# A new plan of order for a fused recurrence and expert kernel, with more buffers and one factor kept in PSUM

## The chip, the cores and the metric

The kernel runs on one core of a Trainium2 chip. The metric is the device time of one execution in microseconds, taken as the median of several runs.

## The reference

Two stages are fused. The first is a gated linear recurrence over 768 steps, for 4 batches and 8 heads with head size 48. The second is an expert layer on the 3072 resulting tokens, with 384 model columns and 2048 hidden columns. All inputs and the output are float32.

```python
f = 1.0 / (1.0 + np.exp(-f_logit))
for t in range(S):
    state = f[:, :, t, :, None] * state + np.einsum('bhd,bhe->bhde', k[:, :, t], v[:, :, t])
    y[:, :, t] = np.einsum('bhd,bhde->bhe', q[:, :, t], state)
x = y.transpose(0, 2, 1, 3).reshape(B * S, H * D)
h = x @ w_in
out = (h * (1.0 / (1.0 + np.exp(-h)))) @ w_out
```

## The kernel before

The sequence is cut into 6 chunks of 128 steps. With 4 batches this makes 24 units, numbered 4 x chunk + batch, each with 128 tokens and all 8 heads. A unit passes through these tasks; the short names are those of the plan and of the function `emit`.

- Inputs: `f`, `k`, `q`, `v` load 128 x 384 float32 each, all issued by SyncE's queue (L156) in 1024 pieces of 192 bytes. `wi` and `wo` (four pieces each, L158 and L160) load and convert the weights from GpSimd's queue.
- Gate: `E` and `L` (ScalarE, L162 and L164) make the logarithm of the gate, with opposite sign; `cs` (TensorE, L167, L171) sums it along the chunk into a PSUM bank; `ia`, `a` and `al` (ScalarE, L174, L176, L178) take exponentials of these sums: the factor for k, the factor for q, and the chunk's decay.
- Scaling: `ki` (GpSimd, L183) multiplies k, `qg` (VectorE, L190) multiplies q, `vb` (GpSimd, L185) converts v.
- Attention inside the chunk: the scaled q and k are transposed, either by TensorE and a copy (`tq`, `qkc`, L195 and L197, 13 units) or by one DMA transpose (`qkD`, L200, 11 units); `sc` (L208) forms scores, `at` (VectorE, L214, two halves) masks them, `y` (L220 with the state, L224 with the scores) gives the output.
- State: `d` (L242), `sd` (VectorE, L247 or L249) and `su` (GpSimd, L254) carry the state to the batch's next chunk. The last chunk skips them.
- Hand-over: `yc` (L228) converts the output, and it is transposed by TensorE (`yT`, `xc`, L232 and L234, 13 units) or by DMA (`yD`, L237, 11 units).
- Expert layer: for each of four parts `mi` (12 matmuls, L260) and `si` (ScalarE, Silu, L266), then `mo` (4 matmuls for each part, L271), `oc` (VectorE eviction, L274) and `so` (store by SyncE's queue, L277).

`T.s` and `T.e` load ScalarE's table for Silu and for the exponentials (L306). `Z.n` runs n matmuls on zeros (L309).

The order of all tasks is written out in the string `PLAN`, made by an offline search. A word is task, unit, part and, behind the colon, the buffer slots that it takes: `mi.3.2:4` is part 2 of unit 3's first expert product into PSUM bank 4. Each engine and each queue runs its own tasks strictly in the plan's order; semaphores for data and for the reuse of buffers are added automatically. `SLOTS` says how many buffers there are of each kind; `ps` are the eight PSUM banks. SyncE's queue holds loads, stores and DMA transposes in one order, so that a store waiting for its `oc` also holds the loads that follow it. A bank taken by `cs` is free for the next taker once its last reader is done.

Of the kernel before, what the change touches and what calls it, by code (L numbers as in the profile page):

```python
# [34 lines left out]
si.0.3:0 T.e yT.4:5 mo.1.0:4 xc.4:1 mo.3.0:6 E.7:1 mi.4.3:0 L.7:0 mi.4.2:1 E.5:0 cs.7:2 mi.4.1:7 L.5:1 f.6:7 al.7:5
ia.7:0 mi.4.0:5 a.7:1 mo.2.1:3 mo.1.1:4 mo.3.1:6 k.6:7 mo.1.2:4 ki.7:0 cs.5:2 v.7:5 mo.2.2:3 al.5:0 ia.5:1 q.6:7
mo.3.2:6 a.5:0 T.s qg.5:3 mo.2.3:3 q.10:0 ki.5:3 mo.3.3:6 oc.2:0 q.8:1 si.4.2:2 mo.1.3:4 qg.7:0 si.4.3:2 oc.3:1 so.2
tq.5:2 si.4.1:2 oc.1:2 v.5:6 tq.7:3 si.4.0:2 T.e qkc.5:1 mo.0.0:1 so.1 qkc.7:2 mo.4.0:0 so.3 vb.7:5 q.9:2 sc.5:6,7
E.6:1 sc.7:4,5 at.5.1:2 d.7:2 L.6:2 mo.0.1:1 f.8:0 at.7.0:0 cs.6:3 at.7.1:0 mo.0.2:1 f.10:1 al.6:3 ia.6:2 at.5.0:2
mo.4.1:0 a.6:2 ki.6:1 v.6:7 sd.7:1 y.7:7 qg.6:1 mo.0.3:1 v.10:0 vb.5:0 yc.7:2 mo.4.2:0 su.7:0 oc.0:3 q.11:3 yT.7:4  # L40
y.5:5 xc.7:2 tq.6:3 so.0 yc.5:0 mi.7.0:6 f.9:2 qkc.6:3 yT.5:2 E.8:0 T.s mi.7.1:7 xc.5:3 v.8:1 mi.7.3:1 k.8:0 mi.5.1:4
si.7.0:1 vb.6:3 mi.5.0:5 v.11:3 si.7.3:1 vb.10:2 si.7.1:1 mi.5.3:3 v.9:2 si.5.1:3 mi.5.2:2 si.5.3:3 f.11:3 mi.7.2:6
si.5.0:3 si.5.2:3 k.9:2 sc.6:1,7 si.7.2:1 T.e mo.4.3:0 at.6.0:1 k.10:1 d.5:4 vb.8:1 at.6.1:1 mo.7.0:3 sd.5:0 k.11:3
d.6:5 y.6:2 E.9:1 oc.4:4 mo.7.1:3 su.5:0 L.8:3 yc.6:1 f.12:4 L.9:4 mo.5.0:6 sd.6:1 vb.11:4 E.10:0 so.4 yT.6:1 cs.8:7
su.6:0 L.10:0 xc.6:0 f.16:5 cs.9:4 mo.5.1:6 al.8:2 ia.8:0 al.9:1 vb.9:5 ia.9:1 f.13:6 mi.6.2:0 ki.8:2 a.9:0 mi.6.3:2
a.8:1 T.s k.13:4 qg.9:4 ki.9:4 mi.6.1:5 qg.8:2 f.14:7 mi.6.0:1 si.6.2:0 v.16:4 tq.8:4 si.6.3:0 tq.9:7 qkc.8:0 si.6.0:0
v.13:5 cs.10:0 si.6.1:0 T.e d.8:2 qkc.9:2 mo.7.2:3 f.15:0 sd.8:0 mo.6.0:1 q.12:4 sc.9:4,5 sc.8:7,2 al.10:4 ia.10:2
at.9.0:0 mo.7.3:3 a.10:2 q.16:5 ki.10:0 at.9.1:0 E.11:1 mo.6.1:1 E.13:0 at.8.0:2 k.12:5 mo.5.2:6 L.11:1 at.8.1:2
L.13:2 y.9:4 v.14:6 vb.16:0 oc.7:5 E.14:1 mo.6.2:1 E.12:0 yc.9:2 so.7 y.8:0 vb.13:3 L.14:3 qg.10:0 cs.13:5 k.16:6
L.12:4 yT.9:7 su.8:0 yc.8:0 cs.11:2 al.13:5 tq.10:3 ia.13:0 xc.9:1 q.15:6 al.11:0 yT.8:4 a.11:0 cs.14:0 ki.13:3  # L50
qkc.10:1 mi.9.2:7 a.13:1 f.17:2 xc.8:3 al.14:3 a.14:2 T.s qg.11:1 mi.9.0:3 k.18:7 mi.8.0:5 mi.8.2:4 q.14:7 si.9.2:2
vb.14:1 si.9.0:2 mo.6.3:1 v.19:7 si.8.2:1 mi.8.1:7 oc.6:6 si.8.0:1 q.13:2 cs.12:3 si.8.1:1 mi.9.1:4 so.6 mi.8.3:1
si.9.1:2 q.17:1 sc.10:5,7 si.8.3:1 mi.9.3:4 v.15:0 at.10.1:1 mo.8.0:1 at.10.0:1 si.9.3:2 T.e k.17:0 mo.5.3:6 qg.14:2
k.14:2 y.10:7 oc.5:7 d.13:5 d.9:4 yc.10:1 mo.8.1:1 al.12:2 so.5 ia.11:1 vb.19:5 sd.9:1 ia.12:2 k.15:1 mo.9.0:6 ki.11:1
E.17:1 qg.13:3 yT.10:7 a.12:0 mo.8.2:1 qkD.13:3 su.9:0 xc.10:2 L.17:0 qg.12:4 tq.11:2 ia.14:0 E.16:0 mi.10.2:4 ki.12:4
qkc.11:2 E.15:1 mi.10.1:3 sd.13:0 L.16:2 T.s q.19:0 tq.12:7 mi.10.0:0 v.21:1 qkc.12:0 ki.14:2 mi.10.3:2 si.10.2:0
f.20:1 si.10.0:0 sc.11:5,7 qkD.14:1 si.10.3:0 d.11:4 at.11.1:0 cs.16:0 mo.8.3:1 si.10.1:0 T.e sd.11:1 sc.13:2,7
at.11.0:0 sc.12:3,4 mo.9.1:6 at.13.0:2 q.20:3 al.16:1 a.16:2 at.13.1:2 y.11:5 L.15:1 mo.10.0:2 v.12:3 yc.11:2 su.11:0
ia.16:1 y.13:7 at.12.1:1 E.20:0 f.18:3 yT.11:5 cs.15:0 vb.21:4 yc.13:0 L.20:3 d.10:4 mo.9.2:6 q.18:7 su.13:0 xc.11:0
al.15:0 a.15:1 sd.10:1 ia.15:2 cs.20:7 yD.13:3 mi.11.2:5 at.12.0:1 a.20:0 su.10:0 ia.20:0 T.s oc.8:0 mi.11.0:4 f.22:6  # L60
qg.16:1 mi.11.3:0 vb.12:3 qg.15:3 so.8 ki.16:1 mi.11.1:3 q.21:2 qg.20:0 si.11.0:3 d.12:7 ki.15:3 si.11.2:3 v.22:2
y.12:1 sd.12:0 mi.13.1:4 si.11.3:3 yc.12:1 qkD.16:2 vb.15:2 si.11.1:3 mi.13.3:5 su.12:0 si.13.1:1 yT.12:7 mi.13.0:0
si.13.3:1 xc.12:1 mi.13.2:1 si.13.0:1 qkD.15:3 vb.22:3 mi.12.1:3 si.13.2:1 T.e mi.12.2:4 mi.12.0:7 mi.12.3:5 E.18:1
v.23:4 E.22:0 mo.11.0:0 v.17:5 L.18:4 mo.9.3:6 L.22:2 T.s k.19:4 mo.11.1:0 oc.9:2 f.21:7 cs.18:1 mo.11.2:0 so.9
si.12.3:2 v.18:6 si.12.1:2 d.15:6 mo.11.3:0 sd.15:1 si.12.0:2 k.22:3 sc.16:5,3 si.12.2:2 T.e oc.11:1 sc.14:6,7 k.21:5
mo.10.1:2 at.16.0:0 at.14.0:2 so.11 sc.15:4,0 f.19:4 mo.10.2:2 at.14.1:2 E.21:1 q.23:4 mo.12.0:5 al.18:5 at.15.0:1
a.18:2 L.21:1 y.14:6 at.15.1:1 q.22:5 ia.18:1 mo.10.3:2 yc.14:2 v.20:7 ki.18:4 y.15:7 at.16.1:0 d.16:4 cs.22:0 yD.14:2
yc.15:0 d.14:1 su.15:0 cs.21:6 a.22:1 y.16:3 sd.16:0 ia.21:2 mo.12.1:5 yD.15:0 yc.16:1 a.21:0 vb.18:2 mo.13.0:7
ia.22:1 sd.14:1 su.16:0 yD.16:3 E.19:0 oc.10:3 cs.17:4 mo.13.1:7 L.19:3 qg.21:3 su.14:0 so.10 al.17:4 qg.22:1
mo.12.2:5 a.17:0 k.20:2 qg.18:4 cs.19:6 vb.17:1 qg.17:2 k.23:6 mo.13.2:7 vb.20:0 al.19:2 a.19:1 T.s ki.22:1 mi.14.1:3  # L70
qkD.18:0 mi.16.2:0 ki.21:3 si.14.1:3 mi.16.0:1 si.16.2:0 ki.20:0 mi.16.3:2 si.16.0:0 qkD.21:1 mi.16.1:3 si.16.3:0
mi.14.0:0 si.16.1:0 mi.14.2:1 si.14.0:3 qkD.20:3 mi.14.3:2 si.14.2:3 qg.19:3 mi.15.3:3 si.14.3:3 T.e mi.15.2:0
mi.15.0:1 qkD.22:2 mo.16.0:2 ia.17:1 ia.19:2 T.s ki.17:2 mi.15.1:4 mo.12.3:5 ki.19:3 f.23:2 mo.13.3:7 oc.12:4
si.15.3:2 mo.16.1:2 si.15.1:2 so.12 oc.13:5 si.15.0:2 sc.20:6,5 so.13 sc.18:3,4 si.15.2:2 T.e at.20.1:2 sc.21:7,1
mo.16.2:2 at.18.0:1 mo.15.0:0 at.18.1:1 mo.16.3:2 at.20.0:2 E.23:1 y.18:5 at.21.1:0 y.20:3 L.23:4 qkD.17:0 yc.18:2
d.18:4 d.17:6 vb.23:0 d.19:1 sd.18:0 mo.15.1:0 sd.17:1 su.18:0 cs.23:5 mo.14.0:4 yc.20:0 ia.23:0 at.21.0:0 a.23:2 T.s
mo.15.2:0 ki.23:0 yD.18:1 sd.19:0 mo.14.1:4 oc.16:6 yD.20:3 qg.23:0 sc.17:6,3 sc.22:5,7 at.17.1:1 mo.15.3:0 so.16
at.17.0:1 qkD.19:3 mi.18.1:1 at.22.0:2 mi.18.3:2 at.22.1:2 mi.18.0:3 si.18.1:1 oc.15:7 si.18.3:1 mi.18.2:6 so.15
si.18.0:1 mi.20.1:5 si.18.2:1 y.17:7 si.20.1:0 mi.20.0:1 yc.17:1 su.17:0 qkD.23:0 mi.20.3:0 si.20.0:0 y.22:2 si.20.3:0
# [263 lines left out]
```

## Time and profile before

| | |
|---|---|
| median of 3 runs | 195.94 us (195.77 to 196.79) |
| the profiled execution: its time / its span | 194.64 us / 192.9 us |
| PE / ACT / DVE / POOL busy | 174.1 / 125.4 / 95.7 / 65.6 us |
| weight loads on PE (PEld) busy | 138.2 us |
| input packets under 512 B | 116544 of 123225 |
| read from HBM / written | 25.17 MB / 4.72 MB |
| granted TensorE clock | 0.997 |

The profile shows one execution. A busy time is the time in which an engine worked on something; PE's includes the overlap of its pipeline. An idle stretch is put down to what ended it. The chain that ended last is followed back from the last instruction, step by step, to what released it; its share of the span was 56% for PE, 17% for DMA, 9% for ACT and 7% for the issue of transfers by SyncE's queue.

### The profile page before, as it was taken

The page shows a single profiled execution, that of the slowest core. Times are in us where ns is not written, and L with a number is a line of the kernel's source. Part 1 is how long each engine was busy: PE and PEld are TensorE (multiplying, and loading weights), DVE is VectorE, ACT ScalarE, POOL GpSimd, SP SyncE. Part 2 cuts the span into 40 slices and gives each one's busy share as a digit, 9 for nine tenths or more (in the row PEclk, how much of TensorE's full clock was granted, in tenths as well). Part 3 has the DMA queues.
Part 4 walks back from the last instruction along what each step waited for, and adds up shares of the span by engine and source line. Part 5 has one row for each costly group of instructions (what it writes and reads, how often), then busy time and mean ns, then how long its engine had stood idle before and what let it go on. Part 6 is the DMA issues. An engine that isn't in the chain of part 4 may idle for free.

```text
span 192.9 us, 5771 instructions
## 1 busy us (share of the span) xinstructions
PE 174.1 (90%) x2397; PEld 138.2 (72%) x2397; DVE 95.7 (50%) x182; ACT 125.4 (65%) x234; POOL 65.6 (34%) x104
## 2 busy tenths in 40 slices
...
GB/s 126 209 196 181 159 202 187 185 185 189 233 224 220 184 222 174 213 200 212 218 209 164 204 177 230 215 133 170 181 114 146 131 76 44 27 57 85 0 82 82
DMA packets 123225, 31.07 MB, mean 161 GB/s; under 512 B 116544, under 2 KB 123200, under 8 KB 123200
## 3 DMA queue, kind: packets, MB, share of 16 engines
...
q0 software_dynamic: 3712, 3.15, 10.3%
...
q14 instruction: 7, 0.06, 0.1%
HBM read 25.17 MB, written 4.72 MB: 155 GB/s over the span
## 4 chain that ended last, share of the span: by engine, by line
PE 56%; DMA 17%; ACT 9%; SPq 7%; issue 4%; POOL 2%; DVE 2%; ACTq 0%; DVEq 0%; POOLq 0%
PE ps L260 25%; PE ps L271 23%; SPq L156 7%; DMA v<-in_v_dram 5%; DMA w_in<-in_moe_w_in_dram 4%; ACT hT L266 4%; DMA xT<-yb 3%; DMA f<-in_f_logit_dram 3%; ACT L306 2%; DMA q<-in_q_dram 2%; PE ps L195 2%; PE ps L208 2%; ACT e L162 2%; PE ps L224 1%; DVE qk L190 1%
## 5 line engine op out<-in xcount | busy, mean ns | idle before, releaser
L266 ACT ACTIVATE hT<-ps 128x512 bf16<-128x512 f32 x96 | 54.1, 599 | 38.1 <-PE ps L260 29.4
L260 PE MATMUL ps<-xT,w_in 128*128 128x128 bf16 x1152 | 70.2, 219 | 4.5 <-DMA xT<-yb 2.1
L260 PEld LDWEIGHTS <-w_in 128*128 128x128 bf16 x1152 | 66.0, 98 | 8.9 <-issue 3.1
L271 PE MATMUL ps<-w_out,hT 128*128 128x384 bf16 x384 | 70.3, 326 | 1.8 <-DVE o L274 1.8
L271 PEld LDWEIGHTS <-hT 128*128 128x128 bf16 x384 | 34.7, 97 | 21.7 <-issue 2.0
L183 POOL TENSOR_TENSOR qk<-k,ia 128x384 bf16<-128x384 f32 x24 | 24.5, 1028 | 36.8 <-ACT ia L174 33.4
L214 DVE TENSOR_TENSOR atm<-ps,triu 128x512 bf16<-128x512 f32 x48 | 30.4, 682 | 12.5 <-PE ps L208 12.5
L190 DVE TENSOR_TENSOR qk<-q,a 128x384 bf16<-128x384 f32 x24 | 18.4, 778 | 26.4 <-ACT a L176 14.7
L254 POOL TENSOR_TENSOR st<-sd,al 48x192 bf16<-48x192 f32 x40 | 21.5, 538 | 24.2 <-PE ps L220 20.9
L274 DVE COPY o<-ps 128x384 f32<-128x384 f32 x24 | 13.2, 554 | 32.4 <-PE ps L271 28.5
L306 ACT ACT_TABLE_LOAD x21 | 26.9, 1283 | 0.4
L185 POOL CAST vb<-v 128x384 bf16<-128x384 f32 x24 | 13.0, 549 | 32.2 <-DMA v<-in_v_dram 25.9
L162 ACT ACTIVATE e<-f 128x384 f32<-128x384 f32 x24 | 12.1, 523 | 9.9 <-DMA f<-in_f_logit_dram 9.9
L228 DVE CAST yb<-ps 128x384 bf16<-128x384 f32 x24 | 13.3, 552 | 7.3 <-PE ps L224 6.1
L174 ACT ACTIVATE ia<-ps 128x384 f32<-128x384 f32 x24 | 11.5, 489 | 1.8 <-POOL st L254 1.8
L176 ACT ACTIVATE a<-ps 128x384 f32<-128x384 f32 x24 | 11.6, 496 | 1.5 <-PE ps L167 1.1
L164 ACT ACTIVATE lf<-e 128x384 bf16<-128x384 f32 x24 | 12.1, 521 | 0.3
L309 PE MATMUL ps<-zero 128*128 128x256 bf16 x70 | 10.8, 300 | 1.1 <-DVE zero L291 1.1
L197 DVE COPY qkT<-ps 128x1024 bf16<-128x1024 bf16 x13 | 8.7, 685 | 4.2 <-PE ps L195 4.2
L167 PE MATMUL ps<-lf,triu 128*128 128x384 bf16 x24 | 7.7, 325 | 3.3 <-ACT lf L164 3.3
L247 DVE TENSOR_TENSOR sd<-ps,st 128x384 f32<-128x384 f32 x16 | 8.7, 550 | 3.0 <-PE ps L242 3.0
L195 PE MATMUL ps<-ident,qk 128*128 128x128 bf16 x104 | 8.2, 219 | 1.8 <-DVE qk L190 1.3
...
## 6 DMA issues: line engine op xcount, KB each, us to landing
...
w_out<-in_moe_w_out_dram POOLq DMA_DIRECT2D x4, 384.0 KB, 11.8
qkT<-qk SPq DMA_TRANSPOSE x11, 4.3
```

The source lines that it names most:

```text
L156: nc.sync.dma_start(out=dst, in_=src)
L162: nc.scalar.activation(take("e", slots[0], "e", u), at("f", u), AF.Exp, scale=-1.0)
L183: nc.gpsimd.tensor_mul(t[:, 1, :, 0:D], at("k", u), at("ia", u))
L190: nc.vector.tensor_mul(t[:, 0, :, 0:D], at("q", u), at("a", u))
L214: nc.vector.tensor_mul(t[:, part], at("sc", part, u).rearrange("p (n c) -> p n c", c=C), triu[:, None, :].to_broadcast([C, NP, C]))
L228: nc.vector.tensor_copy(take("yb", slots[0], "yb", u), at("y", u)[:, 0:HD])
L254: nc.gpsimd.tensor_mul(st[lo:lo + D, :, r * D:(r + 1) * D], sd[lo:lo + D, :, r * D:(r + 1) * D], al[lo:lo + D, :, None].to_broadcast([D, N ...
L260: nc.tensor.matmul(h[:, i, :], w_in_sb[part][:, kk, i * 128:(i + 1) * 128], at("xT", u)[:, kk, :], start=(kk == 0), stop=(kk == KT - 1))
L266: nc.scalar.activation(t[:, 4 * part:4 * part + 4, :].rearrange("p n c -> p (n c)"), at("h", u, part), AF.Silu)
L271: nc.tensor.matmul(at("om", u)[:, 0:d_model], at("hT", u)[:, 4 * part + n, :], w_out_sb[part][:, n, :], start=(part + n == 0), stop=(part ...
L274: nc.vector.tensor_copy(take("o", slots[0], "o", u), at("om", u)[:, 0:d_model])
L306: nc.scalar.preload_act_table_set(SILUS if at_[0] == "s" else EXPS)
```

## The change

The plan is replaced by another one from the same kind of search, whose model lands all transfers later and uses queue rates that were measured. The tasks are the same in number; the order, the choice of units with DMA transposes, the slots and the number of zero matmuls (70 before, 92 after) are different. There are more buffers: 10 instead of 8 of each input, 18 instead of 8 results, one more `qkT` and one more `hT`. The buffers for q's factor (`a`, three of them) are gone: `a` overwrites the sums in their own PSUM bank, and `qg` reads the factor there, so that the bank is held until `qg` has run.

```diff
-SLOTS = {'f': 8, 'k': 8, 'q': 8, 'v': 8, 'e': 2, 'lf': 5, 'ia': 3, 'a': 3, 'al': 6, 'qk': 5, 'vb': 6, 'qkT': 4, 'atm': 3, 'yb': 3, 'xT': 4, 'hT': 4, 'sd': 2, 'o': 8, 'st0': 1, 'st1': 1, 'st2': 1, 'st3': 1, 'ps': 8}
+SLOTS = {'f': 10, 'k': 10, 'q': 10, 'v': 10, 'e': 2, 'lf': 5, 'ia': 3, 'al': 6, 'qk': 5, 'vb': 6, 'qkT': 5, 'atm': 3, 'yb': 3, 'xT': 4, 'hT': 5, 'sd': 2, 'o': 18, 'st0': 1, 'st1': 1, 'st2': 1, 'st3': 1, 'ps': 8}
...
-k.0:0 q.0:0 f.0:0 f.1:1 k.3:1 f.2:2 f.3:3 E.0:0 L.0:0 v.0:0 E.1:1 Z.20:7 cs.0:0 k.2:2 L.1:1 al.0:0 ia.0:0 q.2:1 Z.5:7
...
-qg.3:3 cs.4:3 sc.2:4,6 xc.0:0 q.4:4 al.4:4 ia.4:2 vb.1:1 tq.3:5 at.2.0:1 a.4:2 T.s wi.2 f.7:5 qkc.3:2 wi.1 at.2.1:1
...
-yc.3:1 d.1:6 qkc.1:3 yT.3:0 su.2:0 sd.1:1 Z.3:4 sc.1:7,1 xc.3:1 mi.0.2:3 su.1:0 yc.2:2 at.1.1:0 mi.3.2:4 k.7:5 vb.4:4
...
-at.1.0:0 yT.2:5 si.0.2:0 wi.0 xc.2:2 si.3.2:1 Z.3:2 y.1:6 q.5:5 mi.2.2:0 yc.1:0 wi.3 mi.2.1:2 si.2.2:2 wo.0 k.5:6
...
+k.0:0 q.0:0 k.3:1 k.2:2 f.1:0 f.0:1 f.2:2 q.2:1 f.3:3 E.1:0 L.1:0 k.1:3 E.0:1 Z.31:7 cs.1:0 L.0:1 q.3:2 al.1:0 ia.1:0
+Z.5:7 cs.0:1 E.2:0 a.1 v.0:0 al.0:1 ia.0:1 L.2:2 ki.0:0 f.4:4 a.0 Z.14:7 cs.2:2 E.3:1 qg.0:0 al.2:2 q.4:3 ia.2:2
+ki.1:1 L.3:3 Z.6:7 tq.0:3 a.2 ki.2:2 v.3:1 cs.3:4 qkc.0:0 al.3:3 ia.3:1 qg.2:2 Z.5:1 sc.0:5,6 k.4:4 a.3 vb.0:0
+at.0.0:0 tq.2:7 ki.3:3 d.0:1 at.0.1:0 wi.0 sd.0:0 Z.5:2 y.0:3 f.5:5 E.4:0 qkc.2:1 wi.3 L.4:4 yc.0:0 v.4:2 Z.6:6
+sc.2:2,5 wo.0 qg.3:3 cs.4:6 v.2:3 yT.0:1 at.2.0:1 al.4:4 vb.3:1 tq.3:7 ia.4:0 xc.0:0 su.0:0 a.4 at.2.1:1 d.3:3 sd.3:1
+ki.4:4 q.1:4 qkc.3:2 v.1:4 E.5:1 qg.4:4 su.3:0 Z.13:2 sc.3:4,2 L.5:0 at.3.1:2 tq.4:1 cs.5:5 at.3.0:2 mi.0.0:3 al.5:5
+ia.5:2 qkc.4:3 y.3:7 a.5 T.s yc.3:1 Z.3:4 sc.4:6,2 at.4.0:0 Z.1:1 yT.3:4 xc.3:1 Z.3:7 mi.0.3:1 at.4.1:0 si.0.0:0
+mi.3.0:7 si.0.3:0 v.5:5 mi.3.3:6 vb.4:2 si.3.0:1 wi.2 y.4:4 si.3.3:1 d.4:2 yc.4:2 mo.3.0:3 sd.4:0 f.9:6 vb.2:3 yT.4:1
+mo.0.0:7 su.4:0 xc.4:2 d.2:6 q.5:5 qg.1:1 mi.4.3:4 sd.2:1 wi.1 tq.1:2 si.4.3:2 k.5:5 mi.4.0:1 su.2:0 qkc.1:4 y.2:0
+si.4.0:2 yc.2:0 vb.1:4 sc.1:6,4 at.1.1:2 wo.1 mo.4.0:2 at.1.0:2 yT.2:1 d.1:0 mi.3.2:4 xc.2:3 sd.1:0 mi.4.2:6 si.3.2:1
...
-            nc.scalar.activation(flat(take("a", slots[0], "a", u)), at("cs", u)[:, 0:HD], AF.Exp, scale=-1.0)
+            nc.scalar.activation(at("cs", u)[:, 0:HD], at("cs", u)[:, 0:HD], AF.Exp, scale=-1.0)
...
-            nc.vector.tensor_mul(t[:, 0, :, 0:D], at("q", u), at("a", u))
+            nc.vector.tensor_mul(t[:, 0, :, 0:D], at("q", u), at("cs", u)[:, 0:HD].rearrange("p (h d) -> p h d", d=D))
```

Of the plan only the beginning is shown (for the old one, the lines with the weights). SyncE's queue ends its loads with k.20, k.23, four DMA transposes and f.23 in the old plan, and with f.23, so.13, q.22, so.15 and k.23 in the new one.

More of the change, by code (lines that the diff above doesn't have):

```diff
@@ L35 @@
[L35 to L79, printed above, removed]
@@ L80 @@
-mi.20.2:3 yc.22:2 mo.20.0:6 yD.17:2 si.20.2:0 y.21:5 sc.19:7,1 yD.22:0 yc.21:0 sc.23:0,2 mo.20.1:6 at.19.1:1 yD.21:1
-at.19.0:1 mo.18.0:3 at.23.0:2 mi.17.3:5 at.23.1:2 y.19:1 si.17.3:2 mi.17.0:7 yc.19:1 su.19:0 mi.17.2:0 yD.19:3
-si.17.0:2 mi.17.1:2 si.17.2:2 y.23:5 si.17.1:2 mi.22.1:1 yc.23:2 mi.21.3:7 yD.23:2 mi.19.2:0 mi.19.1:2 mi.19.3:5
-mo.18.1:3 mo.20.2:6 mo.18.2:3 mo.20.3:6 mo.18.3:3 si.19.3:0 oc.20:0 mo.14.2:4 si.19.1:0 so.20 oc.18:2 si.19.2:0
-mi.19.0:6 so.18 si.21.3:1 mi.22.3:5 si.19.0:0 mi.21.1:2 mi.21.2:3 si.21.1:1 mo.19.0:0 si.21.2:1 mo.14.3:4 mi.21.0:7
@@ L85 @@
-oc.14:1 si.22.1:3 mo.19.1:0 si.22.3:3 so.14 si.21.0:1 mi.22.0:6 mo.19.2:0 si.22.0:3 mi.23.1:2 mo.19.3:0 mi.22.2:3
-oc.19:3 si.23.1:0 mi.23.0:4 so.19 si.22.2:3 mi.23.2:1 si.23.0:0 mo.17.0:5 si.23.2:0 mo.21.0:7 mo.17.1:5 mo.21.1:7
-mo.17.2:5 mo.21.2:7 mo.17.3:5 mi.23.3:6 oc.17:4 mo.21.3:7 so.17 si.23.3:0 mo.23.0:0 oc.21:5 mo.22.0:2 so.21 mo.23.1:0
-mo.22.1:2 mo.23.2:0 mo.22.2:2 mo.23.3:0 mo.22.3:2 oc.23:6 so.23 oc.22:7 so.22
+k.0:0 q.0:0 k.3:1 k.2:2 f.1:0 f.0:1 f.2:2 q.2:1 f.3:3 E.1:0 L.1:0 k.1:3 E.0:1 Z.31:7 cs.1:0 L.0:1 q.3:2 al.1:0 ia.1:0
@@ new lines @@
+ia.5:2 qkc.4:3 y.3:7 a.5 T.s yc.3:1 Z.3:4 sc.4:6,2 at.4.0:0 Z.1:1 yT.3:4 xc.3:1 Z.3:7 mi.0.3:1 at.4.1:0 si.0.0:0
+mi.3.0:7 si.0.3:0 v.5:5 mi.3.3:6 vb.4:2 si.3.0:1 wi.2 y.4:4 si.3.3:1 d.4:2 yc.4:2 mo.3.0:3 sd.4:0 f.9:6 vb.2:3 yT.4:1
+mo.0.0:7 su.4:0 xc.4:2 d.2:6 q.5:5 qg.1:1 mi.4.3:4 sd.2:1 wi.1 tq.1:2 si.4.3:2 k.5:5 mi.4.0:1 su.2:0 qkc.1:4 y.2:0
+si.4.0:2 yc.2:0 vb.1:4 sc.1:6,4 at.1.1:2 wo.1 mo.4.0:2 at.1.0:2 yT.2:1 d.1:0 mi.3.2:4 xc.2:3 sd.1:0 mi.4.2:6 si.3.2:1
+k.9:6 su.1:0 mi.0.2:1 si.4.2:2 mi.2.3:0 vb.5:5 si.0.2:0 wo.2 mi.2.0:4 si.2.3:3 mi.3.1:6 si.2.0:3 mi.4.1:1 si.3.1:1
@@ new lines @@
+mi.0.1:0 si.4.1:2 mi.2.1:4 si.0.1:0 mi.2.2:6 si.2.1:3 q.8:6 mo.2.0:1 si.2.2:3 T.e mo.0.1:7 f.6:7 qg.5:0 mo.2.1:1 y.1:0
+E.9:0 mo.3.1:3 yc.1:1 L.9:1 mo.2.2:1 yT.1:4 cs.9:6 k.8:7 ki.5:0 xc.1:1 mo.0.2:7 al.9:1 ia.9:1 mi.1.0:5 a.9 T.s k.7:8
+wo.3 tq.5:0 ki.9:3 mi.1.3:4 f.8:8 qkc.5:0 mo.3.2:3 q.6:7 si.1.0:4 mi.1.2:0 si.1.3:4 mi.1.1:5 si.1.2:4 q.7:8 d.5:4
+mo.4.1:2 si.1.1:4 T.e sd.5:1 q.9:9 mo.1.0:0 sc.5:5,4 mo.1.1:0 at.5.0:0 E.6:1 mo.4.2:2 at.5.1:0 L.6:2 mo.3.3:3 k.6:9
+E.8:0 L.8:3 cs.6:5 oc.3:0 y.5:4 al.6:3 ia.6:0 mo.1.2:0 yc.5:2 su.5:0 so.3 a.6 cs.8:3 f.7:9 mo.0.3:7 qg.6:4 al.8:4
@@ new lines @@
+ia.8:2 yT.5:4 a.8 T.s mo.2.3:1 ki.8:2 oc.0:1 xc.5:2 v.9:6 mo.4.3:2 qg.9:3 oc.2:2 mi.5.1:5 so.0 ki.6:4 oc.4:3 tq.9:7
+so.2 qg.8:2 mi.5.2:4 qkc.9:2 so.4 tq.8:6 f.10:0 si.5.2:1 mi.5.3:1 qkc.8:3 si.5.1:1 mi.5.0:2 si.5.3:1 v.6:7 vb.9:0
+tq.6:3 si.5.0:1 T.e k.10:0 sc.9:7,4 qkc.6:1 v.13:8 d.9:5 mo.5.0:6 at.9.0:1 sc.6:1,2 at.9.1:1 mo.5.1:6 E.7:1 sd.9:0
+E.10:0 y.9:3 v.7:9 at.6.1:2 L.7:4 mo.5.2:6 su.9:0 L.10:0 at.6.0:2 cs.7:7 q.10:0 mo.5.3:6 yc.9:0 al.7:2 ia.7:1 vb.6:1
+cs.10:4 a.7 ki.7:1 v.8:0 oc.5:4 yT.9:5 d.6:2 al.10:0 y.6:1 ia.10:2 xc.9:0 sd.6:1 mo.1.3:0 a.10 T.s ki.10:0 so.5 yc.6:1
@@ new lines @@
+mi.9.3:3 k.17:3 oc.1:5 vb.13:2 yT.6:6 qg.7:1 mi.9.0:5 vb.7:3 xc.6:3 su.6:0 tq.7:2 so.1 qg.10:0 mi.6.3:1 qkc.7:4 q.14:1
+si.9.3:0 tq.10:0 vb.8:4 f.11:1 si.9.0:0 mi.6.2:7 qkc.10:0 si.6.3:3 mi.6.1:6 f.14:2 si.6.2:3 q.12:2 d.7:4 mi.6.0:2
+si.6.1:3 sd.7:0 mi.9.1:3 si.6.0:3 d.8:5 mi.9.2:0 si.9.1:0 sd.8:1 k.11:2 sc.7:1,7 si.9.2:0 T.e mo.6.0:6 at.7.0:0 k.13:1
+at.7.1:0 sc.10:4,2 sc.8:3,5 q.11:3 mo.6.1:6 at.10.1:1 E.14:1 at.8.1:2 y.7:0 E.11:0 k.18:4 mo.6.2:6 at.8.0:2 su.7:0
+L.14:1 mo.9.0:1 L.11:2 at.10.0:1 v.14:1 cs.14:7 yc.7:2 y.8:2 al.14:5 ia.14:0 cs.11:5 k.14:5 yc.8:0 yT.7:3 su.8:0 a.14
@@ new lines @@
+mo.6.3:6 xc.7:1 al.11:1 ia.11:1 qg.14:3 yT.8:4 k.12:6 mi.7.2:0 a.11 T.s ki.11:4 xc.8:2 oc.6:6 mi.7.0:2 f.13:3 qg.11:4
+mi.8.2:3 so.6 tq.11:7 vb.14:5 mi.7.1:4 f.12:4 si.7.0:2 qkc.11:2 si.8.2:1 ki.14:3 mi.8.1:6 si.7.1:2 mi.7.3:5 si.8.1:1
+v.10:2 mi.8.0:2 si.7.2:2 si.7.3:2 qkD.14:1 mi.8.3:7 si.8.0:1 d.14:3 si.8.3:1 T.e sc.11:4,6 mo.8.0:0 at.11.1:0 k.16:7
+mo.7.0:5 at.11.0:0 f.15:5 mo.8.1:0 E.12:1 q.19:4 vb.10:0 E.13:0 mo.7.1:5 L.12:3 y.10:2 f.17:6 L.13:4 mo.7.2:5 yc.10:1
+cs.13:7 cs.12:6 al.13:3 yT.10:4 ia.13:2 f.16:7 mo.7.3:5 xc.10:3 al.12:2 ia.12:1 ki.13:1 d.10:2 a.13 mi.10.1:4 oc.7:7
@@ new lines @@
+q.17:5 a.12 sd.10:0 ki.12:2 E.15:1 T.s mi.10.0:5 qg.12:2 so.7 d.13:2 su.10:0 mo.8.2:0 sd.13:1 tq.12:6 v.11:3 si.10.1:4
+mi.10.3:2 sd.14:0 si.10.0:4 qkc.12:4 mi.10.2:4 v.12:4 si.10.3:4 f.18:8 sc.14:3,5 si.10.2:4 T.e sc.12:6,2 k.19:9
+at.14.0:2 mo.8.3:0 at.14.1:2 mo.9.1:1 oc.8:8 mo.10.0:4 E.17:0 at.12.1:1 so.8 vb.11:1 L.15:0 y.14:3 at.12.0:1 q.13:7
+L.17:1 mo.9.2:1 su.14:0 E.16:1 yc.14:2 cs.15:5 d.11:0 L.16:2 cs.17:2 vb.12:3 y.11:6 al.15:4 yD.14:0 sd.11:0 E.18:0
+cs.16:3 al.17:0 yc.11:0 mo.9.3:1 ia.17:0 su.11:0 al.16:5 ia.16:2 d.12:0 q.16:9 yT.11:6 oc.9:9 a.17 mo.10.1:4 k.15:8
```

38 lines of the change are left out of this document (30 added, 8 removed).

## The prediction, made before the changed kernel ran

> **What bounds the kernel now.** I read the windows first (the busy time of each engine in ten-microsecond stretches; columns after the stretch: its length, PE, PEld, DVE, ACT and POOL busy with counts, then clock, DMA share, GB/s).
>
> ```profile
> 60.00:70.00 10.00, 10.00 (x153) 8.36 (x151) 4.54 (x8) 9.49 (x20) 5.20 (x10) 1.00 0.98 200
> 80.00:90.00 10.00, 9.26 (x144) 7.79 (x141) 2.83 (x7) 9.27 (x19) 2.71 (x4) 1.00 1.04 212
> 90.00:100.00 10.00, 7.85 (x113) 5.97 (x113) 7.62 (x14) 7.25 (x14) 4.96 (x6) 1.00 1.06 211
> 100.00:110.00 10.00, 7.67 (x126) 6.49 (x127) 7.39 (x14) 7.21 (x16) 6.87 (x13) 1.00 1.23 186
> 120.00:130.00 10.00, 8.86 (x109) 6.04 (x109) 8.69 (x15) 8.00 (x18) 7.10 (x11) 1.00 0.84 176
> 150.00:160.00 10.00, 10.00 (x185) 9.08 (x183) 5.14 (x10) 5.24 (x10) 2.01 (x4) 1.00 0.44 92
> ```
>
> PE is full from 25 to 70 us and from 131 to 189; between, it has holes while the DMA share stands at 1. The chain of waits says what the holes wait for:
>
> ```profile
> 12.61 4.73 DMA v<-in_v_dram
> 17.39 0.45 POOL vb L185
> 17.84 7.51 DMA w_in<-in_moe_w_in_dram
> 25.41 1.51 PE ps L260 x24
> ...
> 32.50 2.68 PE ps L260 x48
> ...
> 39.48 1.30 PE ps L271 x8
> ...
> 98.26 5.41 DMA f<-in_f_logit_dram
> 103.75 0.53 ACT e L162
> ...
> 122.94 3.83 DMA q<-in_q_dram
> ...
> 127.77 2.31 DMA xT<-yb
> ```
>
> Two things carry the time: the first expert matmul waits for its weights until 25.41, and later PE waits for inputs that land too late.
>
> To count this, I give each PE task its slot from the same chain: mi 0.67 us (2.68 for four), mo 0.65 (1.30 for two), and likewise tq 0.45, sc 0.30, y 0.21 (0.17 more with a state), yT 0.17, d 0.17, cs 0.16 (0.10 more for its column sums), 0.11 for one zero matmul. Over the plan: mi 64.2, mo 62.4, cs 6.0, tq 5.8, sc 7.2, y 8.4, yT 2.2, d 3.5, zeros 70 x 0.11 = 7.7; sum 167.4. I call lag the start of a PE task less the slots ahead of it in the plan. It is 12.1 at the first mi, still 12.4 at 63 us, 13.4 at 88, 15.2 at 91, 18.7 at 105, 19.7 at 111 and 21.5 from 130 on, 21.7 at the end. So PE keeps to these slots within 0.4 us for 38 us whenever nothing is late, and time = slots + lag + end: 167.4 + 21.7 + 5.5 = 194.6, the profiled execution (5.5 is the last eviction, its store and what lies outside the span of 192.9). The median of the runs shown is 1.3 more.
>
> **The change, part by part.** The tasks are the same in number and kind (13 transposes on PE and 11 by DMA of each sort, 21 table loads); 22 more zero matmuls add 2.4, so the slots become 169.8. The end has the same form (mo, two evictions, two stores), 5.5. All else is the lag.
>
> *Start of the weights.* They sit behind ki.3 on POOL instead of behind vb.1. f.3 is now the ninth input, and the ninth issue was at 7.31. The first f is fifth instead of third: issued at 3.52, landing 3.6 later, so ACT starts at 7.1 instead of 5.46. From there to the end of ia.3 stand 8 exponentials and logarithms, 4 al, 7 ia or a: 8 x 0.55 + 4 x 0.17 + 7 x 0.49 = 8.5, so 15.6; ki.3 takes 1.0, the first issue is at 16.6, the second at 17.4, against 17.84 and 18.7. With the 7.5 us that the first took, and about 9.3 for the one queued behind it, they land at 24.1 and 26.7. Before mi.0.3 stand 16.5 us of slots: lag 10.2, against 12.1.
>
> *The other weights.* They were issued nearly in one burst; now wi.2 stands behind vb.4, wi.1 behind su.4, wo.1 behind su.2 and vb.1, wo.2 behind su.1 and vb.5, wo.3 behind ki.5. POOL's order makes each wait for a state update, so for PE and DVE. d.4 ends near 29.2, sd.4 at 30.5, su.4 at 31.6: wi.1 issues at 31.7. Alone on its queue it takes between 5.5 (my estimate from the 7.5 row, less the 2 us for traffic ahead) and 7.7 (the page's median), so 37.2 to 39.4; mi.3.1 has 27.3 ahead, so it asks for it at 37.5. That is a lag of 10.2 to 12.1. wo.2 issues near 37 and lands at 43 to 45; mo.2.2 has 33.5 ahead: lag 10 to 11.5. I take 11.5 leaving this stage; at 11.8 us, the page's median for w_out, it would be 16.
>
> *Inputs against PE work.* Here the plan changes most. From the queue's own timeline
>
> ```profile
> 45.08 1.02 SPq L156 DMA_DIRECT2D k<-in_k_dram  x1
> 84.87 1.02 SPq L156 DMA_DIRECT2D k<-in_k_dram  x1
> ```
>
> (k.6 and k.18) 36 inputs and 6 stores took 39.8 us: with 0.6 for a store, 1.0 an input; a DMA transpose is about 1.3. Ahead of f.20 stood 74 inputs, 8 stores, 1 transpose, 80 us; now 79, 11 and 5, 92 us: 12 later. But PE work ahead of cs.20, its first use, goes from 86.2 to 110.6, 24.4 more. f.20 thus gains 12.5 us of lead. In the same way f.19 gains 15 (8 against 23.2) and f.23 13.5 (0.5 against 14.0). The lateness that built up between 70 and 130 us was 9.4 of lag, so I take it out. Ten slots instead of eight keep SP's order from waiting on a consumer; 18 result buffers take the store's landing out of the eviction's way; the fifth qkT and hT free two more reuses. In before's waits of PE none of these reuses stands, so they are nothing by themselves: they let the new order run. Check: f.6 is the 28th input as k.6 was, so near 45; f.20 is 52 inputs, 11 stores, 5 transposes on, 110; its use less landing 4.1 and 1.1 on ACT is 110.6 + 12 - 5.2 = 117. The 7 us are mostly eaten by SP standing in order for oc, qg, ki and yc of the stores and transposes ahead, but those waits move with PE. What the path finds next is PE itself, and the transposes of units 21 to 23 (3 to 4 us each from issue) near the end, with next to no slack; I give 1 to 2 us for them and for thin spots.
>
> *q's factor in PSUM.* Three effects. DVE:
>
> ```profile
> L190 DVE TENSOR_TENSOR qk<-q,a x24: 543/576/1350, 8.4 to 147.1; 128x384 bf16<-128x384 f32 x24
> L247 DVE TENSOR_TENSOR sd<-ps,st x16: 543/548/558, 32.6 to 146.2; 128x384 f32<-128x384 f32 x16
> ```
>
> The form with an operand in PSUM never stretches, so 24 x (778 - 548) ns = 5.5 us less on DVE, which is half idle: counted as nothing. ACT: the built order shows that a, overwriting its bank, now waits for ACT's own ia, which before it only followed:
>
> ```profile
> 12.87 0.49 ACT L174 ACTIVATE ia<-ps 128x384 f32<-128x384 f32 x1
> 13.24 0.50 ACT L176 ACTIVATE a<-ps 128x384 f32<-128x384 f32 x1
> ```
>
> 0.37 from start to start becomes about 0.55, as between e and lf (which waits so): 24 x 0.18 = 4.3 on ACT. Writing to PSUM is in no row of ACT; bounds: 0.1 less each, or twice the streaming time, 0.33 more (496 ns for 384 columns less 168 for 4), so -2.4 to +8. I take 0, as source and shape are those of the row of 496. The Trainium skill (ScalarE: Activation LUTs, Step-by-step) says ACT writes PSUM faster than SBUF, but that this only helps where TensorE doesn't need most of PSUM; by its first half the sum would not move, its second half is a rival below. ACT is at 9.3 to 9.5 of 10 between 60 and 90, yet at 105 us of PE work 93 us of ACT work are now ahead instead of 101, so I count 0.5 of the 4.3. Banks: a cs bank was free after a, 1.7 us of PE work after cs on average; now after qg, 6.7 on average. The plan leaves 0.7 to 3.9 us of PE work from qg to the bank's next matmul, which covers a DVE of 0.55: nothing, if q is in time.
>
> Sum of the lag: 11.5 + 1.4 + 0.5 = 13.4. Time 169.8 + 13.4 + 5.5 = 188.7 by the profile, 190.0 as median.
>
> **The rivals.** (1) The weights come late, each at 7.7 to 11.8 us behind a state update: lag 16 to 18, 192.6 to 194.6. For it: the links su-weight on POOL; against: total traffic up to 45 us is unchanged. (2) ACT pays the upper bound in its full stretch, 4 to 5 us, 194.5. For it: ACT's share; against: the smaller ACT work ahead. (3) The lead does not come out, since SP's order still waits on late evictions and yc, and the stalls merely move: lag 19 to 20, 196, no change. (4) Slower: the banks. A late q or a busy DVE holds qg, qg holds a cs bank, and PE, in order, stands at that bank's next matmul. It decides from 24 x 0.3 us: then the lag is over 20; at 0.45 each it is 11 more, 24, so 200.8. For it: in the weights' stretch q.5 took 16.6 us from issue to landing, and all eight banks are in use; against: most q's are issued well ahead. The Trainium skill's second half, above, would speak for this one; no run here shows it yet.
>
> **How the numbers follow.** Forecast, lag 11.5 to 15.5: 0.68 (188.1 to 192.1). Rival 1: 0.12, rival 2: 0.07, rival 3: 0.05, rival 4: 0.08. The range takes the forecast's and rival 1's cases and, below, a lag of 10.4 (the first stage's best with no thin spots): 187.0 to 195.0. What a measurement can tell from no change is 0.5%, about 1 us. Faster: 0.68 + 0.11 + 0.04 = 0.83; same: 0.06; slower: 0.11.
>
> **What would show it.** The first mi near 24 us and mi.0.3 near 26.7; PE full from there with less than 3 us of holes; no long piece of f or v in the chain after 45 us; L190 near 548 with no stretch; f.20 landing before 118; slots still at 0.67 and 0.65. I am wrong if PE waits for w_out or w_in at 37 to 50 us (rival 1), if L176 reads over 0.7 us (2), if the DMA of an f or v still ends PE's waits (3), or if PE's waits name L190 (4).

## The result and the profile after

| | before | after |
|---|---|---|
| median of 4 runs each | 196.37 us (195.77 to 198.82) | 188.36 us (187.63 to 189.29) |
| the profiled execution: its time / its span | 194.64 / 192.9 us | 188.93 / 187.0 us |
| PE / ACT / DVE / POOL busy | 174.1 / 125.4 / 95.7 / 65.6 us | 176.0 / 127.4 / 90.6 / 62.6 us |

The ratio of the times is 0.9605, with a 95% interval of 0.9532 to 0.9677: 4% faster. The ratios here leave slower, disturbed executions out, so that a median over all runs need not follow its ratio, and the profiled executions of three experiments (extra loads, three; old plan with fewer loads; weights and tail moved) were such ones, read for where waits stand and how the lag grows within them, not for their time.

The windows of the new kernel come first, in the columns of the prediction (PE, PEld, DVE, ACT and POOL busy, clock, DMA share, GB/s).

```profile
90.00:100.00 10.00, 10.00 (x143) 7.81 (x141) 7.53 (x14) 8.98 (x19) 4.35 (x7) 1.00 1.20 222
100.00:110.00 10.00, 10.00 (x174) 9.02 (x172) 4.61 (x10) 9.38 (x21) 5.50 (x9) 1.00 1.05 167
120.00:130.00 10.00, 10.00 (x170) 9.00 (x169) 4.13 (x9) 8.20 (x13) 2.01 (x4) 1.00 0.86 174
150.00:160.00 10.00, 9.62 (x127) 6.76 (x126) 6.25 (x13) 4.54 (x7) 2.59 (x4) 1.00 0.85 179
```

Where PE was busy for 7.85, 7.67 and 8.86 of ten microseconds it is now full, with about the same share of the DMA engines in use. The holes that are left stand in the chain of waits (start, length, what):

```profile
16.21 10.84 DMA v<-in_v_dram
...
27.17 0.51 POOL vb L185
...
29.80 0.45 POOL st L254
30.25 8.36 DMA w_in<-in_moe_w_in_dram
...
148.47 4.11 DMA xT<-yb
152.62 1.51 PE ps L260 x24
```

The first stage still waits for transfers: v.4 takes 10.84 us beside the first weights, vb.4 and the state update of unit 4 follow, and only then POOL issues wi.1, which takes 8.36; PE waits 1.2 us for it at 38.66. From 45 us on, one DMA transpose near the end is the only transfer in the chain. Counted in lag:

| PE task | lag before (at) | lag after (at) |
|---|---|---|
| first mi | 12.05 (25.41 us) | 8.55 (22.92 us) |
| mo.2.2, the weights' stage done | 12.27 (46.43) | 11.35 (44.82) |
| mi.16.2, behind the late inputs | 21.53 (130.12) | 12.32 (126.08) |
| the last tasks | 21.7 to 21.9 | 13.5 to 13.7 |

In the middle stretch, from mo.2.2 to mi.16.2, the lag grew by 9.3 and now grows by 1.0, which is 8.3 less; the weights' stage adds 0.9 to that and the tail takes 1.0 back, so 8.2 us of lag are gone. The 22 further zero matmuls cost 2.4 in slots, the end 0.1: 8.2 - 2.5 = 5.7, the difference of the two profiled executions. The ratio is worth more, about 7.8 us of the kernel before: its profiled execution (194.64) was faster than each of its four runs in the table. The 2 us between the two are not explained by this count, and no run here was made for them.

### The profile page after: what moved, and what is told of

It is laid out like the page before. It is cut to its first block, busy times and chain, and to the rows that moved or that the text cites. A ratio compares the mean times of both kernels' runs of the same rounds, so it can differ in the third digit from the quotient of the medians.

```text
span 187.0 us, 5803 instructions
## 1 busy us (share of the span) xinstructions
PE 176.0 (94%) x2419; PEld 140.1 (75%) x2419; DVE 90.6 (48%) x182; ACT 127.4 (68%) x234; POOL 62.6 (33%) x104
## 4 chain that ended last, share of the span: by engine, by line
PE 75%; DMA 12%; SPq 8%; issue 1%; DVE 1%; POOL 1%; DVEq 0%; POOLq 0%
PE ps L260 31%; PE ps L271 31%; SPq L156 8%; DMA v<-in_v_dram 6%; DMA w_in<-in_moe_w_in_dram 4%; PE ps L208 3%; PE ps L224 2%; DMA xT<-yb 2%; PE ps L195 2%; PE ps L220 2%; PE ps L167 1%; PE ps L242 1%; PE ps L232 1%; DVE o L274 1%; PE ps L171 1%
## 5 line engine op out<-in xcount | busy, mean ns | idle before, releaser
L266 ACT ACTIVATE hT<-ps 128x512 bf16<-128x512 f32 x96 | 55.6, 598 | 27.8 <-PE ps L260 21.9
L260 PE MATMUL ps<-xT,w_in 128*128 128x128 bf16 x1152 | 71.2, 219 | 2.0 <-DMA w_in<-in_moe_w_in_dram 1.6
L271 PE MATMUL ps<-w_out,hT 128*128 128x384 bf16 x384 | 71.6, 326 | 0.2 <-ACT hT L266 0.2
L183 POOL TENSOR_TENSOR qk<-k,ia 128x384 bf16<-128x384 f32 x24 | 23.7, 998 | 32.5 <-ACT ia L174 20.3
L254 POOL TENSOR_TENSOR st<-sd,al 48x192 bf16<-48x192 f32 x40 | 20.1, 502 | 39.3 <-PE ps L220 27.5
L190 DVE TENSOR_TENSOR qk<-q,ps 128x384 bf16<-128x384 f32 x24 | 13.0, 547 | 17.0 <-ACT ps L176 11.0
L185 POOL CAST vb<-v 128x384 bf16<-128x384 f32 x24 | 12.0, 506 | 23.5 <-DMA v<-in_v_dram 23.1
L309 PE MATMUL ps<-zero 128*128 128x256 bf16 x92 | 13.5, 298 | 1.1 <-DVE zero L291 1.1
L176 ACT ACTIVATE ps<-ps 128x384 f32<-128x384 f32 x24 | 11.8, 498 | 0.0
L309 PEld LDWEIGHTS <-zero 128*128 128x128 bf16 x92 | 9.1, 106 | 2.8 <-DVE zero L291 1.1
```

Of the source, the lines that this page charges most:

```text
L183: nc.gpsimd.tensor_mul(t[:, 1, :, 0:D], at("k", u), at("ia", u))
L190: nc.vector.tensor_mul(t[:, 0, :, 0:D], at("q", u), at("cs", u)[:, 0:HD].rearrange("p (h d) -> p h d", d=D))
L254: nc.gpsimd.tensor_mul(st[lo:lo + D, :, r * D:(r + 1) * D], sd[lo:lo + D, :, r * D:(r + 1) * D], al[lo:lo + D, :, None].to_broadcast([D, N ...
L260: nc.tensor.matmul(h[:, i, :], w_in_sb[part][:, kk, i * 128:(i + 1) * 128], at("xT", u)[:, kk, :], start=(kk == 0), stop=(kk == KT - 1))
L266: nc.scalar.activation(t[:, 4 * part:4 * part + 4, :].rearrange("p n c -> p (n c)"), at("h", u, part), AF.Silu)
L271: nc.tensor.matmul(at("om", u)[:, 0:d_model], at("hT", u)[:, 4 * part + n, :], w_out_sb[part][:, n, :], start=(part + n == 0), stop=(part ...
```

## The experiments

The theory is the prediction's: the gain is the order of transfers against PE work, inputs with more lead; buffers and the place of q's factor give nothing by themselves. The rivals are that the buffers, or the factor in PSUM, carry the gain, or that it is the weights' stage. The chips of these runs were about 1% slower (the kernel before had medians of 198.2 to 198.5 us there), so ratios to its runs beside them are compared, not times.

**New plan with the old number of input and result buffers.** All slot numbers of inputs and results are assigned anew; the order stays, and so do the fifth `qkT` and the fifth `hT`.

```diff
-'f': 10, 'k': 10, 'q': 10, 'v': 10, ... 'o': 18
+'f': 8, 'k': 8, 'q': 8, 'v': 8, ... 'o': 8
```

> The new plan with the old buffer counts for the four inputs and the result (8 each); tasks and order are unchanged, only slot numbers are given anew, each load taking the buffer that came free longest ago. Theory (the order of transfers against PE work gives the gain): in the plan's order at most 6 buffers of a kind are in use at once, so 188 to 190, no DMA wait that the new plan doesn't have, ratio to before 0.955 to 0.97. Rival (the extra buffers let SyncE's queue run ahead and are the gain): 193 to 196, with SyncE waiting on consumers before loads.

Measured: 191.03 us, ratio 0.9626 (0.954 to 0.9712). Nearly the whole gain is there without the buffers. Its profiled execution (191.41 us) leaves the weights' stage with a lag of 11.17, as the new kernel does, and ends at 16.06 against 13.7, with two small waits for DMA transposes, 0.56 us in unit 17 and 0.73 in unit 15, that the new kernel hasn't. Both also stand, with 0.16 and 0.40 us, in the kernel with q's factor in SBUF, which has all the buffers, so they need not come from the buffers; up to 2 us may hang on those, which the intervals don't tell apart.

**Old plan with the new buffers.** The mirror image; `qkT` and `hT` keep their four.

```diff
-'f': 8, 'k': 8, 'q': 8, 'v': 8, ... 'o': 8
+'f': 10, 'k': 10, 'q': 10, 'v': 10, ... 'o': 18
```

> The old plan with the new buffer counts for inputs (10) and results (18), slots given in turn by which came free first. Theory (order): 195 to 197, the lag still jumps at 88 to 98, 103 to 109 and 127 to 130 us, ratio 0.99 to 1.01. Rival (buffers): 189 to 192.

Measured: 198.86 us, ratio 0.9976 (0.9902 to 1.0049): nothing. The jumps of the lag stand at the same tasks as before (mo.9.0 +2.5, cs.20 +1.3, mi.16.2 +1.3), and the window of the late inputs is as empty as it was:

```profile
90.00:100.00 10.00, 7.50 (x85) 6.09 (x85) 5.80 (x10) 6.12 (x14) 4.94 (x6) 0.83 0.97 203
```

The buffers alone are no cause.

**New plan with q's factor in SBUF.** `a` writes eight buffers of its own again.

```diff
-            nc.scalar.activation(at("cs", u)[:, 0:HD], at("cs", u)[:, 0:HD], AF.Exp, scale=-1.0)
+            nc.scalar.activation(flat(take("a", slots[0], "a", u)), at("cs", u)[:, 0:HD], AF.Exp, scale=-1.0)
```

> The new plan, but q's factor goes to buffers of its own (8) as before, and the bank is free after it. Theory (order): within 1 us of the new kernel, 187.5 to 189.5; q's scaling takes 700 to 800 ns again on average with stretches over 1 us, VectorE is 4 to 5 us busier, PE does not wait for it. Rival (the factor in PSUM gives the gain through VectorE and GpSimd): 191 to 196.

Measured: 189.53 us, ratio 0.9562 (0.9489 to 0.9635); span 187.1, last lag 13.71. The rows of L190 in the new kernel and in this one (least, median and longest in ns):

```profile
L190 DVE TENSOR_TENSOR qk<-q,ps x24: 544/545/555, 12.0 to 151.3; 128x384 bf16<-128x384 f32 x24
```

```profile
L190 DVE TENSOR_TENSOR qk<-q,a x24: 543/610/1346, 12.3 to 151.5; 128x384 bf16<-128x384 f32 x24
```

With the factor in SBUF the stretch up to 1.35 us is back (690 ns on average, a little less than expected), and VectorE is busy for 93.6 us against 90.6, GpSimd for 66.6 against 62.6. The time doesn't follow: both engines have room.

**Old plan with q's factor in PSUM.** In the old plan `a` runs ahead of `ia` for units 11, 14 to 20 and 22; there k's factor is now taken from sums that `a` has already overwritten, so this kernel changes that part of the computation and is read for its time alone. For units 3, 4, 7, 10, 13, 15, 16 and 18 the old plan also gives the bank to another PE task before `qg` has read the factor; `qg` then reads what that task left, and the task doesn't wait for it. So the hold on the bank is tried in the other 16 units only.

```diff
-            nc.scalar.activation(flat(take("a", slots[0], "a", u)), at("cs", u)[:, 0:HD], AF.Exp, scale=-1.0)
+            nc.scalar.activation(at("cs", u)[:, 0:HD], at("cs", u)[:, 0:HD], AF.Exp, scale=-1.0)
```

> The old plan with q's factor written over the sums in PSUM. Theory (order; this plan frees the bank after the factor, so now PE stands at banks where q's scaling comes late): 196 to 200, q's scaling at 545 to 560 ns without stretches, PE's waits name it or ScalarE. Rival (factor in PSUM gives the gain): 189 to 193.

Measured: 199.08 us, ratio 1.0048 (0.9963 to 1.0134). L190 reads 543/548/555 ns there too. PE's waits name it:

```profile
PE ps L242 <- DVE qk L190: 0.4, 1, 0.4
...
PE ps L260 <- DVE qk L190: 0.2, 1, 0.2
PE ps L208 <- DVE qk L190: 0.2, 1, 0.2
```

These are d.12, mi.0.1 and sc.22, each at a bank that `qg` of another unit (20, 4 and 23) still had to read. So the mechanism of rival 4 exists in this plan, at 0.9 us in all. In neither plan does the factor's place move the time by more than the intervals, in the old one as far as this kernel holds the banks.

**Old plan, two weight loads earlier.** wi.2 and wi.1 move to where the new plan puts its first weights, right behind ki.3 on POOL's queue.

```diff
-... ki.3:3 tq.2:1 ... T.s wi.2 f.7:5 qkc.3:2 wi.1 at.2.1:1
+... ki.3:3 wi.2 wi.1 tq.2:1 ... T.s f.7:5 qkc.3:2 at.2.1:1
```

> The old plan with the first two weight transfers ahead of vb.1 and vb.3 on GpSimd instead of behind vb.1. Theory (up to 105 us the first stage sets the lag, behind it the landing of inputs does): the issue moves from 17.8 to about 14.6 and the first expert matmul from 25.4 to 22 to 23.5, the lag there falls by 2 to 3, but cs.20 starts where it did (104 to 105.5) and the total changes by less than 1 us, ratio 0.994 to 1.006. Rival (PE alone bounds, the lag of the start passes through to the end): 2 to 3 us faster, ratio 0.985 to 0.99.

Measured: 199.94 us, ratio 1.0096 (1.0042 to 1.015): about 1% slower. Theory and rival both missed. Its chain of waits:

```profile
15.04 8.99 DMA k<-in_k_dram
24.11 0.99 POOL qk L183
...
28.93 5.40 DMA w_in<-in_moe_w_in_dram
```

The early weights share the DMA engines with the inputs of the first units; k now takes 8.99 us, ki and the first state updates wait for it, and the weight behind them waits for those. The first mi starts at 26.66 instead of 25.41, and the lag behind the weights' stage is 14.3 instead of 12.3. Earlier weights are paid for by later inputs here. This would fit a stage that is bound by its total traffic, but the lag got worse by 2 us with the same traffic, so the order counts too, and no run separates the two.

**Fewer loads, in the old and in the new plan.** The loads of q for units 8 to 23 are left out; those units read unit 5's q, so the output is another one.

```diff
-        if kind in SRC:
+        if kind == "q" and u >= 8:
+            where[kind, u] = where[kind, 5]
+        elif kind in SRC:
```

> The old plan without the q loads of units 8 to 23 (these units scale the q of unit 5), 16 of 96 inputs and about 16 us of transfers less. Theory (late landings make the old plan's holes between 70 and 130 us): the jumps of the lag at 98 to 130 us shrink to 1 to 2 us in all, the last lag falls from 21.7 to 13 to 16, time 6 to 8 us less, ratio 0.96 to 0.97. Rival (ScalarE at over 90% or the banks make those holes): less than 2 us gained, ratio over 0.99.

> The new plan without the same 16 q loads (units 8 to 23 scale the q of unit 5). Theory (after the first stage the new plan's inputs land in time for PE, its lag is 11.3 at 39 us and 13.5 at the end): at most 1.5 us less than the new kernel, ratio to before 0.95 to 0.96. Rival (the new plan too is still held by its inputs): 4 to 6 us less, ratio 0.93 to 0.94.

Measured: the old plan 187.67 us, ratio 0.94 (0.9311 to 0.949), more than expected. Its holes are closed:

```profile
90.00:100.00 10.00, 9.85 (x145) 7.63 (x144) 7.90 (x15) 9.91 (x20) 4.96 (x6) 1.00 0.81 166
100.00:110.00 10.00, 9.83 (x174) 8.94 (x173) 8.16 (x15) 9.35 (x20) 8.18 (x14) 1.00 0.77 129
```

Behind the first stage its lag grows by 2.4 (15.15 at 49 us, 17.5 at the end) instead of 9.4. So what the old plan lost between 70 and 130 us was late inputs, and 16 of 96 loads fewer give it back, or more. (This run has less traffic, not another order; that another order does it with the same traffic is what the new plan shows.) The new plan: 188.96 us, ratio 0.9493 (0.9429 to 0.9557), just below what the theory gave. In its profiled execution the last lag is 13.66 and the pieces of the chain lie 0.1 us from those of the new kernel at 106 and 124 us: no input holds the new plan there. The ratio is about 1% under that of the new kernel (0.9605, and 0.9647 below), so in other executions inputs may cost it up to 2 us or 3; no run here tells.

**How much room the new plan has.** Three or eight further loads of f into buffers that nobody reads, ahead of k.16 on SyncE's queue.

```diff
-at.11.1:0 k.16:7
+at.11.1:0 D.8 k.16:7
...
+            elif kind == "D":
+                for _ in range(int(at_[0])):
+                    nc.sync.dma_start(out=spare[_], in_=SRC["f"].rearrange("b h s d -> s b h d")[0:C, 0])
```

> The new plan with 3 more input loads (f of unit 0 into buffers that nobody reads) in SyncE's queue ahead of k.16, at about 87 us: all later inputs come some 3 us later. Theory (inputs land 1 to 2 us ahead of where PE needs them, no more, since SyncE stands in order for stores and transposes): 1 to 2 us slower than the new kernel, ratio to before 0.965 to 0.975. Rival (the 12 us of lead that the count of transfers ahead gave are free): no change, ratio under 0.962.

> The same with 8 more loads, some 8 us. Theory (1 to 2 us of slack, waits of SyncE absorb some more): 3 to 6 us slower than the new kernel, ratio to before 0.975 to 0.99, with new waits of PE behind 100 us. Rival (12 us of lead): less than 1 us, ratio under 0.965.

Measured: three loads 196.25 us, from 191.71 to 199.44, too wide for a ratio, so that the price of three loads stays open; the lag jumps by 2.2 at mi.10.2. Eight loads 198.62 us, ratio 1.0048 (0.999 to 1.0106), the lag jumping by 7.28 at the same task. For eight loads the theory's price was too low: the whole gain is lost. SyncE's queue, ScalarE and PE's longest wait in the kernel with eight:

```profile
86.54 8.18 SPq L310 DMA_DIRECT2D spare<-in_f_logit_dram  x8
```

```profile
100.24 0.52 ACT L163 ACTIVATE e<-f 128x384 f32<-128x384 f32 x1 [7.51 <-DMA f<-in_f_logit_dram]
100.78 1.28 ACT L307 ACT_TABLE_LOAD   x1
```

```profile
PE ps L261 <- ACT hT L267: 7.3, 1, 7.3
```

E.15 waits 7.51 us for f.15. Behind it in ScalarE's order stand T.s and the Silu of unit 10, which has nothing to do with f.15; PE waits for the bank that this Silu must read, 7.3 us. With 8.18 us of queue added and 7.3 arriving at PE, about 0.9 us was room; with three loads (3.1 us at the same rate) 2.2 arrive, again 0.9. The last lag is 24.1 with eight loads, so 10.4 were lost for 8.2 added; where the rest went stands in the last section.

**Two attempts to go further.** First, wi.1 right behind wi.2, wo.1 behind su.4 and wo.2 behind vb.1 on POOL, and mo.14.3 and mo.17.3 ahead of mi.20.0 on PE, as work to cover unit 20's transpose; then the second part alone.

```diff
-mi.20.0:3 qkD.22:2 mi.20.3:6 mo.14.3:5 ... si.20.3:0 mo.17.3:7 at.19.1:0
+mo.14.3:5 mo.17.3:7 mi.20.0:3 qkD.22:2 mi.20.3:6 ... si.20.3:0 at.19.1:0
```

> The new plan with three GpSimd moves (wi.1 directly behind wi.2, wo.1 behind su.4, wo.2 behind vb.1) and with mo.14.3 and mo.17.3 ahead of mi.20.0 on PE. Theory (lag: 9.9 to 11.3 is the wait for wi.1, the wait for unit 20's transpose adds about 0.8): 1 to 2.5 us less than the new kernel, last lag 11 to 12.5, ratio to before 0.945 to 0.955. Rival (the first stage is bound by all transfers together, so that earlier weights only delay the inputs beside them): the lag at mi.3.1 stays at 11, and only the tail's 0.8 is gained, ratio 0.955 to 0.96.

> The new plan with mo.14.3 and mo.17.3 moved ahead of mi.20.0 on PE, the rest unchanged. Theory (PE stands 0.8 us at mi.20.0 for unit 20's transpose, with work that could be done meanwhile): 0.5 to 1 us less than the new kernel, last lag 12.4 to 13. Rival (the next transposes or ScalarE take the place): within 0.3 us of it.

> The new kernel once more, beside the other kernels of this call on the same chip: ratio to before 0.955 to 0.966, last lag 13 to 14.

Measured: both parts 191.51 us, ratio 0.9511 (0.9391 to 0.963); the tail alone 189.91 us, 0.9624 (0.9562 to 0.9685); the new kernel beside it 190.44 us, 0.9647 (0.9581 to 0.9712), with a last lag of 15.4 where 13 to 14 was expected. None can be told from the new kernel. With the tail alone the wait at mi.20.0 shrinks by 0.3 us and comes back at sc.23. The weights' part met an execution in which f.5, issued at 15.39, landed only at 26.29; in the new kernel's two profiled executions it was issued at 14.72 and 15.22 and landed at 21.51 and 23.42. The lag at cs.5, which needs it, was 13.3, 8.6 and 10.5 in the same order. How f.5 meets the first weights differs from one execution to the next by some 5 us of lag at this point; that this makes the spread among runs fits these three, and no run was made for it alone.

What the experiments leave together is the plan as a whole. It also changes which units use DMA transposes, the PSUM slots, the order of PE's own tasks, the zero matmuls and the fifth `qkT` and `hT`, and no run takes these apart from the order of the loads.

## Why the prediction was right, point by point

*The time.* 190.0 was forecast as median and 188.7 by the profile; 188.36 and 188.93 were measured. The profile was met to 0.2 us; the allowance of 1.3 from profile to median didn't show. The lag was forecast at 13.4 and measured at 13.5 to 13.7. That it is so close is partly luck: terms below are off in both directions. And the gain was forecast too small, 5.9 us (195.94 to 190.0) for about 7.8.

*Inputs against PE work* was the term that carries the forecast, 9.4 us of lag, and it holds: 9.3 of growth became 1.0. The two kernels with fewer loads show that late inputs were the old plan's loss and are not the new plan's. The check on f.20 failed: it was to land before 118 and landed at 119.88; E.20 took it at 119.90 and cs.20 started at 122.80, with no wait on PE. My time of need, 117, was some 3 us too early, since I carried over 5.2 us from landing to use, where 2.9 were enough. The sentence that the lead is mostly eaten by SyncE standing in order was right, and more so than it reads: f.20 issued at 116.35, six later than its place in the queue alone would give, and of the 12.5 us "gained" the extra loads found 0.9 at f.15.

*Start of the weights.* mi.0.3 was forecast at 26.7 with a lag of 10.2, and came at 25.16 with 8.67: wi.0 issued at 15.52 instead of 16.6, and took 6.2 us instead of 7.5. What held PE was then no longer a weight: wi.0 was there at 21.69 and wi.3, which mi.0.3 needs, at 24.11, and neither mi waited. The lag stood at 8.6 from cs.5 on (22.66), which waited for f.5, landed at 21.51. The forecast had this step as a wait for weights. *The other weights* ate the gain of this step: wi.2, which I had counted as issued well before wi.1, sat behind v.4 until 27.63, and wi.1 took 8.36 us where I had 5.5 to 7.7. The lag at mi.3.1 was 11.34 for a forecast of 11.5, by two errors that cancelled. Rival 1 described the mechanism of this stage (a weight at 7.7 to 11.8 us behind a state update), and its sign, a wait of PE for w_in between 37 and 50 us, came (1.2 us at 38.66); it was wrong in its total.

*The thin spots.* 1.4 and 0.5 were counted behind that stage, 1.9; 2.2 to 2.3 were lost. PE's waits in the new kernel (total, times, longest; the first row belongs to the weights' stage):

```profile
PE ps L260 <- DMA w_in<-in_moe_w_in_dram: 1.6, 2, 1.2
...
PE ps L260 <- DMA xT<-yb: 0.4, 1, 0.4
```

Only the 0.4 for unit 20's transpose is a wait of this stretch. The rest comes in steps of less than 0.15 us, where tasks take a little more than their slots; the sum had no term for that, and the total was met by an allowance meant for other things.

*q's factor.* L190 at 545 ns with no stretch, as forecast, and the freed time on VectorE is worth nothing, as the kernel with the factor in SBUF shows. ScalarE's self-wait was mis-sized: 0.18 us for each of 24 was counted on ScalarE, from 0.37 start to start to 0.55. The timeline after shows

```profile
13.82 0.48 ACT L174 ACTIVATE ia<-ps 128x384 f32<-128x384 f32 x1
14.19 0.50 ACT L176 ACTIVATE ps<-ps 128x384 f32<-128x384 f32 x1
```

0.37 still, here and in all 16 pairs that follow each other directly. The 4.3 us on ScalarE don't exist, and the 0.5 that I let through had nothing behind it. Writing to PSUM costs ScalarE 498 ns for 496, between my bounds and at the value taken. The Trainium skill (ScalarE: Activation LUTs, Step-by-step) calls PSUM the faster destination; this shape shows no difference.

*The rivals.* The banks (4) didn't come in the new plan: no wait of PE names L190 there. In the old plan with the factor in PSUM they came three times, with 0.9 us in all, far from the 24 x 0.3 that would have decided, though that kernel holds the bank in 16 units only. ScalarE's upper bound (2) fell with the 498 ns. The stalls that merely move (3) are refuted by the full windows, though the thin room shows how near it was: three loads more, and they are back.
